# Attention beside an MLP on one core: one visit of the small tiles per slot, and q and k fetched by squares of 32

## The chip, the cores and the metric

The kernel runs on one core of a Trainium2 chip. A core has a matrix engine (TensorE, in the profile PE, with its weight loads as PEld), three other compute engines (VectorE = DVE, ScalarE = ACT, GpSimd = POOL), SyncE (SP), whose queue issues nearly all DMAs here, and 16 DMA engines. The metric is the time of one execution on the device in microseconds; the kernel before has a median of 1464.3 us in 11 runs, from 1461.86 to 1468.6.

## The reference

Eight batches, 12 heads, 448 tokens, head width 64. q and k are normalised by their root mean square along the head width and multiplied by a vector each; then ordinary attention; then an MLP without bias, whose activation is h - tanh(h).

```python
def rmsnorm(x, g):
    rms = np.sqrt(np.mean(x * x, axis=-1, keepdims=True) + 1e-06)
    return x / rms * g
q_n, k_n = (rmsnorm(q, g_q), rmsnorm(k, g_k))
scores = 1.0 / np.sqrt(64) * np.matmul(q_n, k_n.transpose(0, 1, 3, 2))
attn = np.exp(scores - np.max(scores, axis=-1, keepdims=True))
attn = attn / (np.sum(attn, axis=-1, keepdims=True) + 1e-09)
x = np.matmul(attn, v)                    # (8, 12, 448, 64) -> (3584, 768)
h = x @ w_in                              # 768 -> 2048
out = (h - np.tanh(h)) @ w_out            # 2048 -> 768
```

All of it is float32. The two weight matrices come as float64 and are rounded to float32 in the kernel.

## The kernel before

The work of attention is cut into 48 steps: 8 batches by 6 pairs of heads. The MLP works on one whole batch at a time. It needs all six pairs of a batch, so it runs one batch behind: while batch b of the MLP is computed, the attention of batch b + 1 is computed in six *slots* (function `slot`, one for each step s). The MLP is a generator, `mlp()`, that issues one matmul at a time; `run(ns)` takes as many matmuls from it as are worth that time. A slot issues a few pieces of attention, calls `run`, issues the next pieces, and so on: the order in which instructions are written down is the order in each engine's queue, and nothing reorders them later. All six slots of a batch run the same amount of the MLP, four gaps (`gap_ns`). The batch's hidden layer (`hidden`) falls into its first three slots, the projection (`project`) into its last three.

The MLP's two products use seven block products instead of eight, each on blocks of half the rows and half the tokens (224): in the hidden layer a product is 6 matmuls of 128x128 by 224 columns, in the projection 8. Each product fills one of three `mm` banks; VectorE, ScalarE and GpSimd add, subtract and apply tanh. From the second batch on the blocks of weights are read back from DRAM through a ring of six places (`ring_load`, L382 and L384), up to five products ahead.

In the steady part, what a slot s does for attention is spread over four steps:

- **fetch** (L99 to L114, SP's queue): q and k of step s + 4, v of step s + 2. A partition holds several rows of q in one piece of 1024 bytes; k comes in pieces of 256 bytes, three rows to a partition and a rest of 64 rows that is loaded twice.
- **norm**, step s + 3: squares on ScalarE (L119, L120); sums on VectorE (L129, L130); power -1/2 on GpSimd (L131), 8 columns for q and 8 for k; q is scaled on VectorE (L400). k is not: its factor is the `scale` of the exp later.
- **turn**, step s + 2: 8 transposes on TensorE (L411 for k, L415 for q) into two banks, and two copies on ScalarE (L413, L419) to kT and qT.
- **scores** of step s + 1 (L438) and their exp on ScalarE (L443). There are three chunks of 128 keys (0, 1, 2) and one of 64 (`KF`); two heads sit in two halves of the rows of TensorE, 64x128 tiles. Chunks 0 and 1 are in a visit at the slot's start; `KF` and chunk 2 in the middle of the slot.
- **values and sums** of step s, in the same middle visit: last keys (L477, 64x32 tiles), sums of probabilities (L510), values of three chunks (L489, 128x32 tiles), reciprocal (L515) and division (L523) on VectorE.

A *visit* is a stretch in which TensorE is taken from the MLP's 128x128 tiles to smaller ones. Scores, sums and values share five `sc` banks (sc_157 to sc_161 in the rows below), taken in turn; a bank is free when ScalarE or VectorE has read it. The probabilities of a step are also added up on VectorE (`add`, L459 and L460, `add_last`, L467), so that the sums need four matmuls.

Of the kernel before, what the change touches and what calls it, by code (L numbers as in the profile page):

```python
# [91 lines left out]

def fetch(nc, name, t, pair):

# [9 lines left out]
    if name == "v":  # L104
        last = t[:, :, KF]
        nc.sync.dma_start(
            out=t[:, :, :KF].rearrange("p h c d -> p h (c d)"), in_=full.rearrange("h p c d -> p h (c d)")
        )
    else:
        last = t[:, KF]  # L110
        for h in range(2):
            nc.sync.dma_start(out=t[:, :KF, h], in_=full[h])
# [21 lines left out]
def bounded_path(tc, ctx, q, k, v, moe_w_in, moe_w_out, out, g_col, ident, ones, half_ones, neg_half, early):  # L134
# [69 lines left out]
    def load(s, names):  # L204
        b, hp = steps[s]
        for name in names:
            src = {"q": q, "k": k, "v": v}[name]
            if s == 0 and name != "v":
                t = early[name]
            else:  # L210
                shape = [CP, 2, NCH, D] if name == "q" else [P, NCH, 2, D] if name == "k" else [P, 2, NCH, D]
                t = nat.tile(shape, F32, name=f"{name}_nat", bufs=3 if name == "v" else 2)
                fetch(nc, name, t, src[b, 2 * hp : 2 * hp + 2])
            loaded[name, s] = t
# [191 lines left out]
    def turn(s, tk, tq):  # L406
# [13 lines left out]
        turned[s] = rr, kT, qT  # L420

    def sc_bank():
        return bank_of("sc")

    def scores(s, c):
# [16 lines left out]
        for h in range(2):  # L442
            nc.scalar.activation(  # L443
                p[:, h, c if c < 2 else 0, :], tiles[h][:, :n], AF.Exp, scale=rr[:, 0, 2 * c + h : 2 * c + h + 1]
            )
# [221 lines left out]
    def store(b, n, y):  # L667
# [4 lines left out]
        o = part("th").rearrange("p f s -> p (f s)")  # L672
        nc.vector.transpose(out=o, in_=y.rearrange("r (c p) -> r p c", c=NCH))
        for i in range(P // BL):
# [41 lines left out]
    def project_first(b):  # L716
# [35 lines left out]
        wp_stack.close()  # L752
        late["tg"] = pool("tg", bufs=1)

    def mlp():
# [64 lines left out]

    def slot(s):
        gap = gap_ns(s)
        if s < 2 * NP:
            totals(s, sc_bank())
        if has(s + 1):
# [12 lines left out]
        if has(s + 1):  # L838
            scores(s + 1, KF)
        dn = sc_bank() if s >= 2 * NP else None  # L840
        av = [sc_bank() for _ in range(2)]
        last_values(s, av)
        if s >= 2 * NP:
            totals(s, dn)
        divide(s, values(s, av))
        if has(s + 1):
            scores(s + 1, 2)
        for work, n in ((add, 1), (add_last, 1), (norm, 3), (norm_q, 3)):
            run(gap / 2)
            if has(s + n):  # L850
                work(s + n)

    load(0, "qk")
    load(1, "qk")
# [4 lines left out]
    for s in range(NP, NS):  # L859
        slot(s)  # L860
    run(1e9)
# [345 lines left out]
```

## Time and profile before

| | |
|---|---|
| median of 11 runs | 1464.3 us |
| the profiled execution | 1465.15 us, span 1463.4 us |
| PE busy | 1430.6 us, 10272 matmul records |
| DVE, ACT, POOL busy | 818.1, 456.3, 511.6 us |
| DMA | 267895 packets, 250.74 MB, mean 171 GB/s |
| packets under 512 B | 164724 |

The page has the busy time of each engine, a chain of work that ended last (followed back from the last instruction), groups of instructions by line with their mean time, and DMA issues. A float32 matmul appears as two records of the same line. In a row of groups the fields are line, engine, operation, output and inputs, shapes, count, then busy us and the mean of one in ns, then the idle time in front of it and what ended it. In a row of the timeline or the chain they are start and length in us.

### The profile page before, as it was taken

How to read it: one execution, taken by the hardware profiler on the slowest of the kernel's cores; microseconds unless marked ns; L12 is line 12 of the kernel's file. 1: busy time of each engine (PE TensorE's matmuls, PEld its weight loads, DVE VectorE, ACT ScalarE, POOL GpSimd, SP SyncE). 2: the span in 40 equal slices, each digit the busy share in tenths (PEclk: the TensorE clock that was granted, in tenths of full speed). 3: DMA queues.
4: the chain of work that ended last, by engine and by line, in shares of the span. 5: the costliest groups of instructions: out<-in, count | busy, mean ns of one | idle time of the engine just before them, and what ended most of it. 6: DMA issues, size and time to landing. Idle time of an engine off the chain costs nothing.

```text
span 1463.4 us, 26034 instructions
## 1 busy us (share of the span) xinstructions
PE 1430.6 (98%) x10272; PEld 1187.5 (81%) x10272; DVE 818.1 (56%) x1246; ACT 456.3 (31%) x850; POOL 511.6 (35%) x378
## 2 busy tenths in 40 slices
PE   6999899999999999999999999999999999999997
PEld 3568654488888888888888888888888888889997
DVE  4999888755553665347535554555554366433322
ACT  6755453233222332223322233213322233201100
POOL 4656465224331334214422243322433133312310
PEclk9999899999999999999999999999999999999999
DMA  8769778855566555655555545555546654555663
GB/s 188 172 186 265 246 191 225 228 171 156 167 161 171 165 151 160 173 155 155 175 161 163 162 150 177 160 142 170 172 151 165 168 163 139 149 164 162 183 193 98
DMA packets 267895, 250.74 MB, mean 171 GB/s; under 512 B 164724, under 2 KB 210036, under 8 KB 267764
## 3 DMA queue, kind: packets, MB, share of 16 engines
q1 hardware_dynamic: 267760, 248.97, 59.8%
q8 instruction: 84, 1.38, 0.4%
q14 instruction: 47, 0.39, 0.1%
q10 hardware_dynamic: 4, 0.00, 0.0%
HBM read 215.48 MB, written 33.42 MB: 170 GB/s over the span
## 4 chain that ended last, share of the span: by engine, by line
PE 91%; DVE 3%; DMA 2%; ACT 2%; SPq 1%; issue 1%; POOL 0%; ACTq 0%; DVEq 0%
PE mm L578 65%; PE sc L438 9%; PE sc L489 6%; PE mm L743 4%; PE sc L510 2%; PE sc L477 1%; PE sc L411 1%; PE sc L415 1%; DMA w_raw<-in_moe_w_out_dram 1%; DVE rs L515 1%; DVE w_out L82 1%; PE mm L489 0%; DMA q_nat<-in_q_dram 0%; ACT p L443 0%; DMA k_nat<-in_k_dram 0%
## 5 line engine op out<-in xcount | busy, mean ns | idle before, releaser
L578 PE MATMUL mm<-xT,w_f 128*128 128x224 f32 x1392 | 278.8, 355 | 0.0
L578 PEld LDWEIGHTS mm<-xT,w_f 128*128 128x128 f32 x1392 | 260.3, 190 | 16.9 <-issue 9.8
L578 PEld LDWEIGHTS mm<-gT,w_f 128*128 128x128 f32 x1344 | 251.4, 190 | 22.5 <-issue 15.3
L578 PE MATMUL mm<-gT,w_f 128*128 128x224 f32 x1344 | 267.7, 355 | 0.0
L131 POOL TENSOR_TENSOR rr<-rr,neg_half 112x8 f32<-112x8 f32 x96 | 156.5, 1650 | 204.8 <-DVE rr L130 202.9
L615 POOL TENSOR_TENSOR gT<-s,th 128x448 f32<-128x448 f32 x96 | 121.0, 1265 | 297.5 <-ACT th L614 296.8
L578 PE MATMUL mm<-tt,w_f 128*128 128x224 f32 x1044 | 211.2, 354 | 0.0
L578 PEld LDWEIGHTS mm<-tt,w_f 128*128 128x128 f32 x1044 | 196.1, 190 | 7.8 <-issue 7.8
L578 PE MATMUL mm<-tg,w_f 128*128 128x224 f32 x1008 | 200.4, 353 | 0.0
L578 PEld LDWEIGHTS mm<-tg,w_f 128*128 128x128 f32 x1008 | 189.5, 190 | 0.0
L438 PE MATMUL sc<-qT,kT 64*128 64x448 f32 (+1 forms) x960 | 172.4, 503 | 12.0 <-ACT p_last L443 8.5
L443 ACT ACTIVATE p<-sc,rr 128x448 f32<-128x448 f32 x192 | 106.0, 638 | 203.5 <-PE sc L438 203.5
L538 POOL TENSOR_TENSOR tt<-xT,tt 128x224 f32<-128x224 f32 x23 | 31.3, 1363 | 290.8 <-DVE xT L523 290.8
L438 PEld LDWEIGHTS sc<-qT,kT 64*128 64x128 f32 (+1 forms) x960 | 62.9, 167 | 80.4 <-issue 62.0
L515 DVE RECIPROCAL rs<-sc 128x224 f32<-128x224 f32 x42 | 65.4, 1557 | 77.5 <-PE sc L510 77.4
L443 ACT ACTIVATE p_full<-sc,rr 128x448 f32<-128x448 f32 x96 | 55.9, 631 | 144.1 <-PE sc L438 144.1
L614 ACT ACTIVATE th<-s 128x448 f32<-128x448 f32 x96 | 55.4, 577 | 100.7 <-DVE s L640 55.6
L489 PE MATMUL sc<-p,v_nat 128*32 128x224 f32 x1344 | 79.1, 353 | 0.0
L743 PE MATMUL mm<-gT,w_out 128*128 128x448 f32 x192 | 77.0, 558 | 0.0
L697 DVE TENSOR_TENSOR s<-mm,s 128x224 f32<-128x224 f32 x21 | 8.2, 391 | 116.8 <-PE mm L578 109.4
L443 ACT ACTIVATE p_last<-sc,rr 128x224 f32<-128x224 f32 x96 | 37.8, 447 | 114.4 <-PE sc L438 114.4
L523 DVE TENSOR_TENSOR xT<-sc,rs 64x224 f32<-64x224 f32 x168 | 65.3, 389 | 10.3 <-PE sc L489 2.2
(123 smaller groups left out, 1631.7 us busy)
## 6 DMA issues: line engine op xcount, KB each, us to landing
w_f<-w_in SPq DMA_DIRECT2D x196, 384.0 KB, 3.5
w_f<-w_out SPq DMA_DIRECT2D x147, 512.0 KB, 4.2
w_raw<-in_moe_w_out_dram SPq DMA_DIRECT2D x16, 768.0 KB, 5.1
out_dram<-th SPq DMA_DIRECT2D x192, 56.0 KB, 2.0
q_nat<-in_q_dram SPq DMA_DIRECT2D x47, 224.0 KB, 4.4
v_nat<-in_v_dram SPq DMA_DIRECT2D x48, 192.0 KB, 3.7
k_nat<-in_k_dram SPq DMA_DIRECT2D x94, 96.0 KB, 2.8
w_in<-w_out SPq DMA_DIRECT2D x21, 384.0 KB, 6.2
```

The lines of the kernel that those rows point to most:

```text
L131: nc.gpsimd.tensor_tensor(out=r, in0=r, in1=neg_half[:rows], op=ALU.pow)
L438: nc.tensor.matmul(tiles[h][i * keys : (i + 1) * keys, :n], lhsT=kT[r, c * P : c * P + keys], rhs=qT[r, i * n : (i + 1) * n], start=True, ...
L443: nc.scalar.activation(p[:, h, c if c < 2 else 0, :], tiles[h][:, :n], AF.Exp, scale=rr[:, 0, 2 * c + h : 2 * c + h + 1])
L489: nc.tensor.matmul(av[n][r : r + BL, :HS], lhsT=v_nat[:, h, c, m * BL : (m + 1) * BL], rhs=p[c][:, h, n * HS : (n + 1) * HS], start=False, ...
L510: nc.tensor.matmul(dn[r : r + BL, :HS], lhsT=by[n], rhs=moving[2 * n + h], start=(i == 0), stop=(i == len(parts) - 1),)
L515: nc.vector.reciprocal(rs, dn[:, :HS])
L523: nc.vector.tensor_tensor(out=x[m * D : (m + 1) * D, n * HS : (n + 1) * HS], in0=av[n][m * D : (m + 1) * D, :HS], in1=rs[n * D : (n + 1) * ...
L538: eng.tensor_tensor(out=t2, in0=x22, in1=t1, op=ALU.subtract)
L578: nc.tensor.matmul(bank[:, f * HS : (f + 1) * HS], lhsT=w[:, c * width + f, :], rhs=moving[p](c), start=(first and f == 0 and c == 0), sto ...
L614: nc.scalar.activation(th, h, AF.Tanh, bias=0.0, scale=1.0)
L615: eng.tensor_tensor(out=g[:, rows, cols], in0=h, in1=th, op=ALU.subtract)
L743: nc.tensor.matmul(bank[:, :S], lhsT=w_out_row(f, n // HC)[:, n % HC * P : (n % HC + 1) * P], rhs=g[:, f, :], start=(f == 0), stop=(f == C ...
```

## The change

Two things.

*One visit.* From the third batch's attention on (slots 12 to 47), the new function `slot` issues all four score chunks of step s + 1, the values and sums of step s, in one visit: `KF`, then last keys, sums and values, then chunks 0, 1 and 2. The other pieces follow, with the same four gaps of the MLP between them, cut differently. Slots 6 to 11 keep the old order (`early_slot`).

*Squares.* From the fourth batch on (steps 18 to 47), q and k of a step lie in one tile of 128 partitions by 2 by 14 by 32. Partition group 2h + m (32 partitions) holds half m of the head width of head h; a partition is a token within a block of 32, and there are 14 blocks. It is fetched by eight DMAs of 32x14x32, whose pieces are 128 bytes long. Squares are one instruction on ScalarE (896 columns). VectorE sums 28 groups of 32 columns, copies the other half's sums across (four copies of 32x28), adds, and GpSimd takes the power of 128x28. Then VectorE scales q and k together and turns them with two transposes of 32x32 blocks, which give qT and kT; ScalarE multiplies kT by the vector. k now carries its factor, so the exp's scale is 1. Tokens lie in their natural order, so v is fetched by rows in that order too (two DMAs with pieces of 256 bytes), and the transpose in `store` reads its input straight.

TensorE's queue before, from the turn in a hidden-layer slot up to the middle visit (mm are the MLP's banks, tg its sums of blocks):

```order
L438 MATMUL sc_157<-qT,kT 128x448
L438 MATMUL sc_158<-qT,kT 128x448
L578 MATMUL mm_163<-gT,w_f 128x224 x8
L578 MATMUL mm_164<-tg,w_f 128x224 x6
L411 MATMUL sc_159<-ident,k_nat 128x128 x4
L415 MATMUL sc_160<-ident,n 128x112 x4
L578 MATMUL mm_164<-tg,w_f 128x224 x2
L578 MATMUL mm_162<-tg,w_f 128x224 x8
L578 MATMUL mm_163<-gT,w_f 128x224 x4
L438 MATMUL sc_161<-qT,kT 64x224
L438 MATMUL sc_157<-qT,kT 64x224
```

and now, from the middle of the one visit to the MLP behind it (line numbers of the changed kernel; L551 are the values, L499 the scores):

```order
L572 MATMUL sc_161<-rows,ones 32x224 x4
L551 MATMUL sc_157<-p,v_nat 32x224 x8
L551 MATMUL sc_157<-p_full,v_nat 32x224 x4
L551 MATMUL sc_158<-p,v_nat 32x224 x8
L551 MATMUL sc_158<-p_full,v_nat 32x224 x4
L499 MATMUL sc_159<-qT,kT 128x448
L499 MATMUL sc_160<-qT,kT 128x448
L499 MATMUL sc_161<-qT,kT 128x448
L499 MATMUL sc_157<-qT,kT 128x448
L499 MATMUL sc_158<-qT,kT 128x448
L499 MATMUL sc_159<-qT,kT 128x448
L640 MATMUL mm_164<-xT,w_f 128x224 x2
```

The transposes are gone from the queue, and chunks 0, 1 and 2 stand right behind the values, on the banks of the sums and values of the same visit.

VectorE's queue in a hidden-layer slot before, around the norm (s_ and tg are tiles of the MLP):

```order
L129 TENSOR_REDUCE rr<-n 112x8
L130 TENSOR_SCALAR rr<-rr 112x8
L129 TENSOR_REDUCE rr<-sq 128x8
L130 TENSOR_SCALAR rr<-rr 128x8
L634 TENSOR_TENSOR s_4977<-mm_164,s_4975 128x448
L400 TENSOR_TENSOR n<-q_nat,rr 112x2x4x64
```

and now:

```order
L452 TENSOR_REDUCE rr_mine<-qk_n 128x28
L454 COPY rr_other<-rr_mine 32x28 x4
L455 TENSOR_TENSOR rr_mine<-rr_mine,rr_other 128x28
L456 TENSOR_SCALAR rr_mine<-rr_mine 128x28
L698 TENSOR_TENSOR s_4867<-mm_164,s_4866 128x448
L529 TENSOR_TENSOR rows<-rows,p_last 64x2x224 x2
L677 TENSOR_TENSOR gT<-mm_162,th 128x2x224
L464 TENSOR_TENSOR qk_n<-qk_nat,rr_mine 128x896
L706 TENSOR_TENSOR s_4867<-mm_163,s_4867 128x448
L474 STREAM_TRANSPOSE qT<-qk_n 128x448
```

More of the MLP's additions stand between the sums and the scaling, and the transposes of qT (and, further on, kT) stand among them.

The diff, cut to what the prediction speaks of:

```diff
+    if in_order:
+        for h in range(2):
+            nc.sync.dma_start(out=t[:, h, :KF], in_=pair[h, : KF * P].rearrange("(c p) d -> p c d", p=P))
+    elif name == "v":
...
+    def load_blocks(s):
+        b, hp = steps[s]
+        t = loaded["qk", s] = late["blocks"].tile([P, 2, NJ, BL], F32, name="qk_nat", bufs=2)
+        for i, src in enumerate((q, k)):
+            for h in range(2):
+                rows = src[b, 2 * hp + h].rearrange("(j t) (m d) -> m t j d", t=BL, d=BL)
+                for m in range(2):
+                    r = (2 * h + m) * BL
+                    nc.sync.dma_start(out=t[r : r + BL, i], in_=rows[m])
...
+    def norm_blocks(s):
+        mine, other = (late["blocks"].tile([P, 2 * NJ], F32, name=name, bufs=2) for name in ("rr_mine", "rr_other"))
+        nc.vector.reduce_sum(mine, normed[s].rearrange("p i j d -> p (i j) d"), axis=AX.X)
+        for g in range(P // BL):
+            nc.vector.tensor_copy(out=other[g * BL : (g + 1) * BL], in_=mine[(g ^ 1) * BL : ((g ^ 1) + 1) * BL])
...
+        nc.gpsimd.tensor_tensor(
+            out=mine, in0=mine, in1=neg_half[:, :1].to_broadcast([P, 2 * NJ]), op=ALU.pow
+        )
...
+    def scale_blocks(s):
...
+    def turn_blocks(s, i):
+        n = normed[s][:, i].rearrange("p j d -> p (j d)")
+        if i == 0:
+            qT = qkp.tile([P, S], F32, name="qT")
+            nc.vector.transpose(out=qT, in_=n)
...
+        nc.vector.transpose(out=kT, in_=n)
+        nc.scalar.mul(kT, kT, g_col)
...
-        nc.vector.transpose(out=o, in_=y.rearrange("r (c p) -> r p c", c=NCH))
+        nc.vector.transpose(out=o, in_=y if b >= FIRST else y.rearrange("r (c p) -> r p c", c=NCH))
...
+    def slot(s):
+        gap = gap_ns(s)
+        if has(s + 1):
+            scores(s + 1, KF)
+        dn = sc_bank()
+        av = [sc_bank() for _ in range(2)]
+        last_values(s, av)
+        totals(s, dn)
+        divide(s, values(s, av))
+        if has(s + 1):
+            for c in range(KF):
+                scores(s + 1, c)
+        if has(s + 2):
+            load(s + 2, "v")
+        if by_blocks(s + 3):
+            load_blocks(s + 3)
+        blocks = by_blocks(s + 2)
+        run(gap / 2)
+        if has(s + 1):
+            add(s + 1)
+        if blocks:
+            square_blocks(s + 2)
+        run(gap / 2)
+        if blocks:
+            norm_blocks(s + 2)
+        elif has(s + 2):
+            turn(s + 2, sc_bank(), sc_bank())
...
+        run(gap / 2)
+        if has(s + 1):
+            add_last(s + 1)
+        run(gap / 2)
+        if blocks:
+            scale_blocks(s + 2)
...
+        run(gap / 2)
+        if blocks:
+            turn_blocks(s + 2, 0)
+        run(gap / 2)
+        if blocks:
+            turn_blocks(s + 2, 1)
...
+        run(gap)
...
-        slot(s)
+        (early_slot if s < 2 * NP else slot)(s)
```

46 lines of the change are left out of this document (37 added, 9 removed).

## The prediction

> **What bounds the kernel now.** I read the page first: busy time by engine and the chain that ended last.
>
> ```profile
> span 1463.4 us, 26034 instructions
> PE 1430.6 (98%) x10272; PEld 1187.5 (81%) x10272; DVE 818.1 (56%) x1246; ACT 456.3 (31%) x850; POOL 511.6 (35%) x378
> PE 91%; DVE 3%; DMA 2%; ACT 2%; SPq 1%; issue 1%; POOL 0%; ACTq 0%; DVEq 0%
> ```
>
> TensorE is busy for 98% of the span and is 91% of the chain. An average hides stages, so next the stretches: four slots in the middle of the kernel, inside the part that the change touches.
>
> ```profile
> core 0: us, PE busy (x) PEld busy (x) DVE busy (x) ACT busy (x) POOL busy (x), PEclk, DMA share, GB/s
> 780.00:896.00 116.00, 116.00 (x851) 99.88 (x850) 63.85 (x101) 34.87 (x68) 36.71 (x27) 1.00 0.56 161
> ```
>
> TensorE has no idle time at all in 116 us, at full granted clock; VectorE is busy 55%, ScalarE 30%, GpSimd 32%, the DMA engines 56%. In this stage a microsecond taken off TensorE's stream is a microsecond of the span, as long as nobody else becomes late. So I read one slot in the chain of waits (start us, length us, work, matmul records):
>
> ```profile
> 783.81 1.71 PE sc L438 x8
> 785.51 5.49 PE mm L578 x28
> 791.01 0.44 PE sc L411 x4
> 791.45 0.39 PE sc L415 x4
> 791.83 5.31 PE mm L578 x28
> 797.14 0.54 PE sc L438 x8
> 797.68 0.54 PE sc L477 x16
> 798.22 0.52 PE sc L510 x8
> 798.74 2.27 PE sc L489 x48
> 801.01 0.95 PE sc L438 x4
> 801.96 10.79 PE mm L578 x56
> 812.75 1.71 PE sc L438 x8
> ```
>
> One slot is 812.75 - 783.81 = 28.94 us and only TensorE is on it: scores of two key chunks (1.71), transposes of k and q (L411, L415: 0.83), the long visit (last keys' scores, last values, sums, values, third chunk's scores: 4.82) and 112 matmul records of the MLP (21.6). 28 records take 5.31 us, so a record is 0.19 us.
>
> **Removed from TensorE.** The transposes go in slots 16 to 45, which prepare steps 18 to 47: 30 slots x 0.83 = 24.9 us. I take all of it, because the row behind them (791.83) starts with their end.
>
> The merging removes no matmul. The four-record piece, one pair of chunk scores with one entry and exit, takes 0.95; the eight-record piece takes 1.71. The second pair inside a visit therefore costs 0.76, and the entry and exit 0.95 - 0.76 = 0.19. One visit less is worth 0.19 us in each of slots 12 to 46: 35 x 0.19 = 6.7 us. Below, it is worth nothing if the cost belongs to each change of tile shape inside the long visit; above, not more than the 0.19. I take 0.19.
>
> **Added wait 1: banks.** Scores use five banks in turn. In the long visit they go: last keys A, B; sums C; values D, E; then the three chunks on A B, C D, E A. Before, the first two chunks had a visit to themselves with four banks long free. Who frees them:
>
> ```profile
> 797.73 0.78 ACT L443 ACTIVATE p_last<-sc,rr 128x224 f32<-128x224 f32 x2 [4.15 <-PE sc L438]
> 798.80 1.56 DVE L515 RECIPROCAL rs<-sc 128x224 f32<-128x224 f32 x1 [2.75 <-PE sc L510]
> 800.50 1.65 DVE L523 TENSOR_TENSOR xT<-sc,rs 64x224 f32<-64x224 f32 x4
> 784.85 2.21 ACT L443 ACTIVATE p<-sc,rr 128x448 f32<-128x448 f32 x4 [9.74 <-PE sc L438]
> ```
>
> Put on the clock of this slot, chunk 0 starts at 801.01, where values end; A and B were emptied by 798.51. Chunk 1 starts at 801.77: C is free at 800.36, D after two of the four divisions, 801.33. Chunk 2 wants to start at 802.53: E is free at 802.15, 0.38 us early. Its second matmul needs A again, that is the first exp of chunk 0. The visit at 783.81 shows that exp starting 1.04 us after the scores and taking 2.21 / 4 = 0.55: done at 801.01 + 1.59 = 802.60, 0.07 late. Lower bound 0; upper bound 0.6 if ScalarE has one more exp or tanh of that length in front. Nearest to the row is 0.1: 35 x 0.1 = 3.5 us back.
>
> **Added wait 2: the norms on VectorE and GpSimd.** The rows of the old way, and of operations like the new ones:
>
> ```profile
> L131 POOL TENSOR_TENSOR rr<-rr,neg_half 128x8 f32<-128x8 f32 x48 | 79.3, 1653 | 0.3 <-DVE rr L130 0.3
> L537 POOL TENSOR_TENSOR tt<-xT 128x224 f32<-128x224 f32 x23 | 15.2, 659 | 0.0
> L129 DVE TENSOR_REDUCE rr<-sq 128x8 f32<-128x512 f32 x48 | 32.5, 677 | 1.8 <-ACT sq L120 1.8
> L400 DVE TENSOR_TENSOR n<-q_nat,rr 112x512 f32<-112x512 f32 x47 | 44.6, 949 | 9.1 <-POOL rr L131 8.5
> L673 DVE STREAM_TRANSPOSE th<-s 128x448 f32<-128x448 f32 x48 | 45.1, 939 | 11.9 <-ACT s L749 10.5
> 819.30 0.62 DVE L634 TENSOR_TENSOR s<-mm,s 128x448 f32<-128x448 f32 x1 [4.67 <-PE mm L578]
> 811.87 0.17 DVE L130 TENSOR_SCALAR rr<-rr 128x8 f32<-128x8 f32 x1
> 813.10 0.68 DVE L400 TENSOR_TENSOR n<-q_nat,rr 112x512 f32<-112x512 f32 x1
> 729.68 1.62 DVE L400 TENSOR_TENSOR n<-q_nat,rr 112x512 f32<-112x512 f32 x1
> ```
>
> VectorE now sums 896 columns (677 x 896 / 512 = 1.18 us), does six tiny operations (0.17 each, 1.0), scales 896 columns (0.68 to 1.62 for 512, so 1.2 to 2.8) and transposes twice (0.94 each): 5.3 to 6.9 us against 2.7 before. Its 55% becomes 65 to 70%; that average is no bound. ScalarE saves the copy of qT, and stays under a third.
>
> The power is the open price: 28 columns instead of two instructions of 8. By instruction it is 1.65 us, by column 1.65 x 28 / 8 = 5.8. A 224-column subtraction on GpSimd takes only 0.66, so the 1.65 for 8 columns is hardly a start-up cost; I take 5.5. It does not delay TensorE directly. Behind it: VectorE's scaling waits for it, VectorE's queue behind the scaling holds the additions that empty the MLP's banks, and those TensorE needs.
>
> In program order, with half a gap = 14 records = 2.65 us, the norm stands 5.3 us behind the visit and the scaling at 10.6. On average the sums start at 5.0 and the power at 7.2; it ends at 12.7, so VectorE stands about 2 us, and the scaling ends at 13.9 to 15.5. An MLP addition (0.62) due about 11.7 is then done 2.8 to 4.4 us late. Three MLP banks: a bank is wanted again two products later, in the hidden layer (12 records each) 2 x 2.28 = 4.56 us, in the projection (16 records) 6.1. So it is covered on average, and a product that ends badly waits about 1 us. Bounds: 0, and 1 us in each of the 15 slots that run the hidden layer; I take 0.3 x 15 = 4.5 us. If that cover were gone, the whole stall of VectorE would be TensorE's (first rival). kT is ready at about 19 of 21.2 us before the next visit asks for it.
>
> **The fetch.** Per slot, SP issues eight DMAs of 448 pieces of 128 bytes for q and k instead of five, and v's main fetch becomes two DMAs of 256-byte pieces.
>
> ```profile
> L676 SPq DMA_DIRECT2D out_dram<-th x192: 316/478/1700, 208.8 to 1458.7; - x192
> L112 SPq DMA_DIRECT2D k_nat<-in_k_dram x94: 567/612/1415, 6.4 to 1197.3; - x94
> out_dram<-th SPq DMA_DIRECT2D x192, 56.0 KB, 2.0
> k_nat<-in_k_dram SPq DMA_DIRECT2D x94, 96.0 KB, 2.8
> 1452.00:1454.00 2.00, 2.00 (x12) 2.00 (x11) 0.69 (x2) 0.00 (x0) 0.00 (x0) 1.00 0.75 115
> 706.00:708.00 2.00, 2.00 (x12) 2.00 (x12) 0.11 (x1) 1.76 (x4) 0.69 (x1) 1.00 0.50 114
> ```
>
> The stores of the output have the same shape: 448 pieces of 128 bytes, 0.48 us to issue, 2.0 to land. Where only they move (1452 to 1454), 0.75 x 2 us x 16 engines = 24 engine-us carry 230 KB, about 1800 pieces: 13 ns each. Where fetches of k in 256-byte pieces move (706 to 708), 16 engine-us carry 228 KB, 890 pieces: 18 ns. 3584 pieces at 13 to 18 ns are 47 to 65 engine-us per slot; free are 0.44 x 28.94 x 16 = 204. The issues take 8 x (0.48 to 0.61) = 3.8 to 4.9 us, plus up to 2.5 for v, and queued behind them on SP are the weight loads of the MLP. They stand right behind the visit, so SP works on them while TensorE is in its 6.3 us without need of weights, and loads are asked for up to five products (11 us) ahead. I take nothing; the cost without that cover is the third rival.
>
> **The sum**, against the profiled execution (1465.15 us, the span 1463.4 and 1.75 around it): 1465.15 - 24.9 - 6.7 + 3.5 + 4.5 = 1441.5. That execution lies 0.85 above the median of the 11 runs, 1464.3, so 1441 for a median. A new slot should be 28.94 - 0.83 - 0.19 + 0.1 + 0.15, about 28.2 us.
>
> **The rivals.**
>
> *VectorE is late (slower).* The power takes 5.8 us, waits up to 4 us behind GpSimd's subtractions for gT, and the scaling takes 2.8 as at 729.68. The power then ends near 17, the scaling near 20, and an addition due at 11.7 is 8.9 us late: 4.4 beyond the cover, 15 x 4.4 = 66 us: 1465.15 - 24.9 - 6.7 + 3.5 + 66 = 1503. It decides from a lateness of about 6.7 us, where 15 slots lose the 32 gained. For it: L400 has already waited for the power, 8.5 us in all. Against it: that is under 0.2 us a slot, with only half a gap between power and scaling, where there are now two.
>
> *The banks set the pace (no change).* ScalarE empties a pair in 1.1 us, TensorE fills one in 0.76. If it is behind at the visit's end, with other work in front of the first exp, the last pair loses up to 0.9: 35 x 0.9 = 31.5, and 1465. For it: three pairs now come at once. Against it: five of the six banks are free in time by the rows above.
> The Trainium skill (TensorEngine Tiling (Array Packing), PSUM Bottleneck) warns of this: small tiles speed up TensorE but not the emptying of its banks, which may become the limit. By that rule the merged visit gives back what it saves; the rows give it 0.07 us.
>
> *Short pieces cost more to read than to write (slower).* The DMA engines fill up from (204 + 28 of the old fetches) / 3584 = 65 ns a piece. At 80 ns a slot needs (259 - 28 + 287) / 16 = 32.4 us, where 259 is the 56% of now: 30 x 3.4 above today, 1567. Against it: 13 and 18 ns.
> The Trainium skill (DMA: Bandwidth & Descriptors, Specifications) speaks against the change here: transfers of at least 512 B are needed for line rate, below that there is a read-modify-write. The rows of 128 bytes agree that line rate is missed (115 GB/s at 0.75 share), but a slot has room for it.
>
> *Merging is worth nothing*: each change of tile shape keeps its price, 1465.15 - 24.9 + 3.5 + 4.5 = 1448.
>
> **How the numbers follow.** The forecast has 0.64, its own range 1432 to 1457 (both waits at 0, 1433.5; both near their upper bounds). Merging worth nothing 0.12; late VectorE 0.11; banks 0.08; short pieces 0.05. Within 0.2% (2.9 us, about what can be told from no change) lies most of the banks' case: 0.06. Faster: 0.64 + 0.12 + 0.02 = 0.78. Slower: 0.16. The range 1431 to 1460 leaves out the two slow cases and most of the banks'.
>
> **What would show it.** Slots of about 28.2 us in the chain, with no transposes from slot 16 on and one visit of about 6.4 us; TensorE still without idle time. Right on the banks: chunk 2 follows chunk 1 within 0.1 to 0.2 us. Wrong on VectorE: waits of MLP matmuls for additions behind the scaling, or a power far from 5.5 us. Wrong on the fetch: matmuls waiting for weight loads, or a DMA share near 1. An idle TensorE of over 1 us per slot would overturn the forecast.

## The result, and the profile after

The changed kernel takes 1429.51 us (median of 8 runs, 1426.72 to 1436.29) against 1463.4 us before (median of 31 runs, 1460.47 to 1468.6): a ratio of 0.9772, 95% interval 0.9759 to 0.9785. That is 33.9 us less, where 1441 was forecast; the sign was right, the size too small, and the time lies 1.5 us below the range. The profiled execution took 1429.04 us.

The head of the page after: span, and busy time of each engine with its share of the span and its instructions.

```profile
span 1427.2 us, 25681 instructions
PE 1394.7 (98%) x10032; PEld 1172.9 (82%) x10032; DVE 867.8 (61%) x1396; ACT 412.4 (29%) x790; POOL 531.0 (37%) x348
```

TensorE is as busy as before, 98%, and 35.9 us shorter. VectorE went from 56 to 61%, GpSimd from 35 to 37%, ScalarE from 31 to 29%. The same stretch in the middle as before, with the columns of busy time by engine, granted clock, DMA share and GB/s:

```profile
780.00:896.00 116.00, 116.00 (x842) 102.36 (x841) 74.74 (x124) 30.64 (x62) 52.06 (x30) 1.00 0.64 172
```

There is still no idle time on TensorE in 116 us. Nothing that the change added reaches it here. So the gain must be in the slot itself; the chain of waits after, from one visit to the next (start us, length us, work, records; L499 are scores, L539 last keys, L572 sums, L551 values, L640 the MLP):

```profile
738.84 0.54 PE sc L499 x8
739.38 0.54 PE sc L539 x16
739.91 0.52 PE sc L572 x8
740.43 2.27 PE sc L551 x48
742.70 2.60 PE sc L499 x12
745.29 21.38 PE mm L640 x112
766.68 0.54 PE sc L499 x8
```

A slot is 766.68 - 738.84 = 27.84 us, against 28.94 before and the 28.2 expected. Read in the same way, slot 12 is 28.83, slots 13 to 15 are 28.77 or 28.78, slot 16 (the first that prepares a step by squares) is 27.93, and each of the 29 slots behind it, 17 to 45, is 27.84 or 27.85. The gain is 1.10 us in each of them, in hidden-layer slots and projection slots alike:

| TensorE in one slot, us | before | after |
|---|---|---|
| transposes of k and q | 0.83 | 0 |
| visits (scores, values, sums) | 1.71 + 4.82 = 6.53 | 6.47 |
| 112 records of the MLP | 5.49 + 5.31 + 10.79 = 21.59 | 21.38 |
| slot | 28.94 | 27.84 |

The line on the MLP is the surprise: the same 112 records are 0.2 us shorter. In the rows of before, 28 records behind a visit take 5.49 and 28 behind the turn take 5.31; 56 behind the other visit take 10.79, which is 0.17 more than twice 5.31. The first matmuls behind *each* visit are late by 0.17 to 0.18, and that price, too, is now paid once in a slot instead of twice.

From the first score matmul of slot 12 to the end of the span, before has 1463.4 - 291.83 = 1171.6 us and after 1427.2 - 289.48 = 1137.7, which is 33.9 less. The further 2.3 us by which the two spans differ lie ahead of slot 12, in code that the change leaves as it was; in the profiled executions of eleven kernels that are alike up to there, slot 12 starts between 288.1 and 294.4 us.

The new work on VectorE, GpSimd and ScalarE, by groups (busy us, mean ns of one | idle time in front and its releasers):

```profile
L452 DVE TENSOR_REDUCE rr_mine<-qk_n 128x28 f32<-128x896 f32 x30 | 32.0, 1066 | 0.0
L457 POOL TENSOR_TENSOR rr_mine<-rr_mine,neg_half 128x28 f32<-128x28 f32 x30 | 145.1, 4837 | 256.0 <-DVE rr_mine L456 256.0
L464 DVE TENSOR_TENSOR qk_n<-qk_nat,rr_mine 128x896 f32<-128x896 f32 x30 | 46.4, 1546 | 39.3 <-POOL rr_mine L457 36.7 <-DMA w_f<-w_out 2.6
L474 DVE STREAM_TRANSPOSE qT<-qk_n 128x448 f32<-128x448 f32 x30 | 19.1, 638 | 0.5
L504 ACT ACTIVATE p<-sc 128x448 f32<-128x448 f32 x120 | 55.5, 548 | 109.1 <-PE sc L499 109.1
L504 ACT ACTIVATE p<-sc,rr 128x448 f32<-128x448 f32 x72 | 39.8, 643 | 21.9 <-PE sc L499 21.9
```

The power takes 4.84 us, the sums 1.07, the transposes 0.64. VectorE does stand in front of the scaling for the power, 36.7 us in 30 steps or 1.2 us a step, yet the MLP's matmuls between 500 and 1300 us wait for nobody. The two rows of exp are one operation on one shape: with the factor of k as a column of scales 643 ns, with the constant 1, which the squares make possible, 548.

### The profile page after: what moved, and what is told of

Read it like the earlier page. It is cut to its first block, busy times and chain, and to the rows that moved or that the text cites. A ratio compares the mean times of both kernels' runs of the same rounds, so it can differ in the third digit from the quotient of the medians.

```text
span 1427.2 us, 25681 instructions
## 1 busy us (share of the span) xinstructions
PE 1394.7 (98%) x10032; PEld 1172.9 (82%) x10032; DVE 867.8 (61%) x1396; ACT 412.4 (29%) x790; POOL 531.0 (37%) x348
## 4 chain that ended last, share of the span: by engine, by line
PE 92%; DVE 3%; DMA 2%; SPq 1%; issue 0%; ACT 0%; POOL 0%; ACTq 0%
PE mm L640 66%; PE sc L499 10%; PE sc L551 6%; PE mm L805 4%; PE sc L572 2%; PE sc L539 2%; DMA gT<-in_moe_w_in_dram 1%; DMA w_raw<-in_moe_w_out_dram 1%; DVE w_out L82 1%; DVE rs L577 1%; PE mm L551 1%; DMA q_nat<-in_q_dram 0%; PE sc L419 0%; DVE w_out L78 0%; PE mm L572 0%
## 5 line engine op out<-in xcount | busy, mean ns | idle before, releaser
L640 PE MATMUL mm<-xT,w_f 128*128 128x224 f32 x1392 | 275.6, 354 | 0.0
L640 PEld LDWEIGHTS mm<-xT,w_f 128*128 128x128 f32 x1392 | 262.1, 190 | 9.1 <-issue 7.8
L640 PE MATMUL mm<-gT,w_f 128*128 128x224 f32 x1344 | 263.0, 354 | 0.0
L640 PEld LDWEIGHTS mm<-gT,w_f 128*128 128x128 f32 x1344 | 252.8, 190 | 11.4 <-issue 7.2
L457 POOL TENSOR_TENSOR rr_mine<-rr_mine,neg_half 128x28 f32<-128x28 f32 x30 | 145.1, 4837 | 256.0 <-DVE rr_mine L456 256.0
L640 PE MATMUL mm<-tt,w_f 128*128 128x224 f32 x1044 | 208.7, 353 | 0.0
L640 PEld LDWEIGHTS mm<-tt,w_f 128*128 128x128 f32 x1044 | 197.0, 190 | 3.9 <-issue 3.9
L640 PE MATMUL mm<-tg,w_f 128*128 128x224 f32 x1008 | 197.7, 352 | 0.0
L640 PEld LDWEIGHTS mm<-tg,w_f 128*128 128x128 f32 x1008 | 190.6, 190 | 0.0
L499 PE MATMUL sc<-qT,kT 64*128 64x448 f32 (+1 forms) x960 | 167.7, 499 | 12.2 <-ACT p_last L504 8.6
L499 PEld LDWEIGHTS sc<-qT,kT 64*128 64x128 f32 (+1 forms) x960 | 70.9, 167 | 83.9 <-issue 49.6
L600 POOL TENSOR_TENSOR tt<-xT,tt 128x224 f32<-128x224 f32 x23 | 17.1, 745 | 230.4 <-DVE xT L585 230.4
L504 ACT ACTIVATE p<-sc 128x448 f32<-128x448 f32 x120 | 55.5, 548 | 109.1 <-PE sc L499 109.1
L135 POOL TENSOR_TENSOR rr<-rr,neg_half 112x8 f32<-112x8 f32 (+1 forms) x36 | 59.6, 1678 | 57.1 <-DVE rr L134 57.0
L551 PE MATMUL sc<-p,v_nat 128*32 128x224 f32 x1344 | 79.1, 353 | 0.0
L464 DVE TENSOR_TENSOR qk_n<-qk_nat,rr_mine 128x896 f32<-128x896 f32 x30 | 46.4, 1546 | 39.3 <-POOL rr_mine L457 36.7
L805 PEld LDWEIGHTS mm<-gT,w_out 128*128 128x128 f32 x192 | 36.4, 193 | 37.3 <-issue 36.3
```

What stands on the lines that cost most here:

```text
L135: nc.gpsimd.tensor_tensor(out=r, in0=r, in1=neg_half[:rows], op=ALU.pow)
L457: nc.gpsimd.tensor_tensor(out=mine, in0=mine, in1=neg_half[:, :1].to_broadcast([P, 2 * NJ]), op=ALU.pow)
L464: nc.vector.tensor_tensor(out=n.rearrange("p i j d -> p (i j) d"), in0=loaded.pop(("qk", s)).rearrange("p i j d -> p (i j) d"), in1=rr[:, ...
L499: nc.tensor.matmul(tiles[h][i * keys : (i + 1) * keys, :n], lhsT=kT[r, c * P : c * P + keys], rhs=qT[r, i * n : (i + 1) * n], start=True, ...
L504: nc.scalar.activation(p[:, h, c if c < 2 else 0, :], tiles[h][:, :n], AF.Exp, scale=1.0 if rr is None else rr[:, 0, 2 * c + h : 2 * c + h ...
L551: nc.tensor.matmul(av[n][r : r + BL, :HS], lhsT=v_nat[:, h, c, m * BL : (m + 1) * BL], rhs=p[c][:, h, n * HS : (n + 1) * HS], start=False, ...
```

## The experiments

The theory with which I went to the chip: the gain is made of three parts, 0.83 us per slot for the transposes, 0.17 for one visit instead of two (0.39 saved, less a wait for banks), and 0.09 because the constant scale lets ScalarE give the banks back sooner; the norms and the short pieces cost nothing. Rivals: the squares alone bring all of it, or less than the transposes; the norms have ample room, or none; the fetch is near its limit. The kernel before was timed beside each kernel; its median in the four groups of runs was 1463.1 to 1465.7. No kernel leaves anything out.

**One visit alone.** All steps keep the old fetch, norm and turn.

```diff
-    FIRST, NJ = 3, S // BL
+    FIRST, NJ = B, S // BL
```

> One visit from slot 12 on, but q and k of all batches fetched, normed and turned the old way. Theory: a removed visit is worth 0.20 us where the MLP comes back (its 112 records took 21.59 us a slot before, 21.39 after) plus 0.19 in the visits, less a wait of about 0.22 for banks, as slots 12 to 15 of the changed kernel show (28.77 us against 28.94): 35 x 0.17 = 6 us less than before, about 1457.5 us, slots of 28.77. Rival 1, the prediction's own sum (0.19 less 0.1): 3 us less, 1460. Rival 2, everything beyond the 24.9 us of the transposes is the merging's: 9 us less, 1454.5.

Measured: 1456.71 us, ratio 0.9948 (0.9929 to 0.9967). The chain of waits of one slot (the turn, between the two pieces of the MLP, is left out here):

```profile
495.90 0.54 PE sc L499 x8
...
499.76 2.69 PE sc L499 x12
502.45 5.49 PE mm L640 x28
...
508.77 15.90 PE mm L640 x84
524.67 0.54 PE sc L499 x8
```

A slot is 28.77, 0.17 less than before. The MLP's records take 5.49 + 15.90 = 21.39: one late start, not two, 0.20 saved. The visit takes 502.45 - 495.90 = 6.55 against 6.53. Its three chunks take 2.69, where the prediction's prices make 0.95 + 2 x 0.76 = 2.47; the 0.22 is the loss by the wait for banks, and it eats the 0.19 that the visit saves within itself. So merging is worth what the MLP's side saves: 35 x 0.17 = 6.0 us.

**Squares alone.** Slots 12 to 47 have two visits as before, but norm, scaling and turns are done by squares.

```diff
         if has(s + 1):
-            scores(s + 1, KF)
...
+            scores(s + 1, 0)
+            scores(s + 1, 1)
...
+        run(gap)
+        if blocks:
+            scale_blocks(s + 2)
+        if has(s + 1):
+            scores(s + 1, KF)
+        dn = sc_bank()
+        av = [sc_bank() for _ in range(2)]
+        last_values(s, av)
+        totals(s, dn)
+        divide(s, values(s, av))
+        if has(s + 1):
+            scores(s + 1, 2)
         run(gap / 2)
...
+        if blocks:
+            turn_blocks(s + 2, 0)
...
         if blocks:
-            scale_blocks(s + 2)
+            turn_blocks(s + 2, 1)
```

> Squares from the fourth batch on, but two visits in every slot, as before the change. Theory: 30 slots lose the 0.83 us of transposes and nothing else, 24.9 us less than before, about 1438.5 us, slots of 28.11 us; VectorE's and GpSimd's longer norms cost nothing. Rival 1, the norms do cost and merging repays it: 20 us less or fewer. Rival 2, the squares save more than the transposes: 28 us less, 1435.5.

Measured: 1450.04 us, ratio 0.9906 (0.9887 to 0.9924): 11.5 above what I expected. Projection slots are 28.10, which is 28.94 - 0.84, as they should be; most groups of three hidden-layer slots take 86.85 to 86.90 instead of 3 x 28.10 = 84.3. The chain of waits shows why; from the sums of squares of a step to the scores that need its kT:

```profile
500.14 1.00 DVE rr_mine L452
...
502.46 4.80 POOL rr_mine L457
...
507.28 2.02 DVE qk_n L464
509.30 1.48 DVE rs L577
...
521.27 0.56 DVE kT L478
...
521.85 0.68 ACT kT L479
...
522.57 1.77 PE sc L499 x8
```

Power, scaling, then the reciprocal and the divisions of the middle visit behind the scaling on VectorE, then the turn of k, and the scores at 522.57 wait for kT. In this kernel the norm stood too near the scaling for the visit between. Whether the squares are worth less than the transposes, or my placing of them was bad, this run leaves open; hence the next one.

**Squares alone, with the norm half a slot earlier.** As the one before, but the squares and the norm of step s + 3 follow the middle visit, and the scaling and the turns follow in the next slot.

```diff
         run(gap / 2)
         if blocks:
-            square_blocks(s + 2)
+            scale_blocks(s + 2)
         run(gap / 2)
         if blocks:
-            norm_blocks(s + 2)
+            turn_blocks(s + 2, 0)
...
+        if by_blocks(s + 3):
+            square_blocks(s + 3)
         run(gap / 2)
-        if blocks:
-            turn_blocks(s + 2, 0)
         if has(s + 1):
             add_last(s + 1)
+        if by_blocks(s + 3):
+            norm_blocks(s + 3)
```

> Squares only, two visits in every slot as in the earlier run of squares alone, but each step's norm is made half a slot earlier: sums and power behind the middle visit, scaling and transposes at the start of the next slot, three half gaps apart instead of two, and kT three half gaps and a visit ahead of its use instead of two half gaps. Theory: the 12 us missing there were VectorE's chain through power, scaling, division and transposes, which gave kT 1.1 to 1.3 us late to the next slot's first scores; with room, all slots take 28.11 and the run is 24.9 us below the kernel before, about 1438.5. Rival: the longer norms need the free stretch that one visit leaves; two visits lose about 10 us wherever the norms stand, 1448 or more.

Measured: 1441.57 us, ratio 0.9853 (0.9835 to 0.987). In the chain of waits every slot of that part is now 28.10 or 28.11 us, hidden layer or projection:

```profile
729.74 0.54 PE sc L499 x8
...
734.56 10.79 PE mm L640 x56
...
747.05 10.79 PE mm L640 x56
757.84 0.54 PE sc L499 x8
```

So the squares are worth 0.84 us a slot, the transposes and nothing else: 30 x 0.84 = 25.2 us. By the medians it is 22.2 us, and the interval, 19 to 24, does not hold the 25.2; in the two traces the stretch from the values of slot 11 to those of slot 47 is 25.1 us shorter (1014.2 instead of 1039.3). What the times lack against that must lie outside this stretch or in the spread between executions; which of the two is not shown. The loss of the run before was its placing. Two visits and two late starts of the MLP (10.79 twice) are still there.

**Exp with a column of ones as its scale**, in the changed kernel: the same result, but ScalarE reads the scale from a column again.

```diff
-                scale=1.0 if rr is None else rr[:, 0, 2 * c + h : 2 * c + h + 1],
+                scale=ones[:, :1] if rr is None else rr[:, 0, 2 * c + h : 2 * c + h + 1],
```

> The changed kernel, but the exp takes its scale from a column of ones also where the squares would let it take the constant 1. Theory: the last pair of scores waits for the first exp of the visit, and an exp with a column takes 0.64 us instead of 0.55; the twelve records of chunk scores go from 2.60 to 2.69 us, a slot from 27.84 to 27.93: 30 x 0.09 = 2.7 us more, about 1432. Rival: the pair waits for VectorE's divisions alone, 2.60 stays, no change.

Measured: 1430.25 us, ratio 0.9769 (0.9746 to 0.9793). Against after that is 0.7 us more by the medians, within the noise of the times; the trace decides. The group of the exps, and then the three chunks in the chain of waits of this kernel:

```profile
L504 ACT ACTIVATE p<-sc,ones 128x448 f32<-128x448 f32 x120 | 66.2, 634 | 103.8 <-PE sc L499 103.8
```

```profile
742.93 2.69 PE sc L499 x12
```

The exp is 0.09 longer, the chunks take 2.69 instead of 2.60, and all slots are 27.93 or 27.94. What ScalarE loses on its first exp TensorE loses in full: the wait for banks is a wait for ScalarE, and the constant scale is worth 30 x 0.09 = 2.7 us.

**Fetch twice.** Each of the eight DMAs of q and k is issued a second time, into a tile that nobody reads.

```diff
-                    nc.sync.dma_start(out=t[r : r + BL, i], in_=rows[m])
+                    for dst in (t, more):
+                        nc.sync.dma_start(out=dst[r : r + BL, i], in_=rows[m])
```

> The changed kernel with each of the eight fetches of q and k issued twice, the second into a tile that nobody reads. Theory: the fetch is covered with room for as much again: within 3 us of 1429.5, with a DMA share higher by about a tenth in the slots. Rival, short pieces come near the limit of the DMA engines or of SP's queue: matmuls wait for weight loads, some 30 x 1 us or more.

Measured: 1429.65 us, ratio 0.9768 (0.9749 to 0.9787), slots 27.84 or 27.85. The stretch in the middle, with the columns as above:

```profile
780.00:896.00 116.00, 116.00 (x842) 102.36 (x841) 74.14 (x125) 30.61 (x62) 51.58 (x30) 1.00 0.73 190
```

The share goes from 0.64 to 0.73. In a slot that is 0.09 x 27.84 x 16 = 40 engine-us for 3584 more pieces, about 11 ns each. The fetch has room even twice over.

**The power twice**: a second power of the same 28 columns stands in front, its result unused.

```diff
-        nc.gpsimd.tensor_tensor(
-            out=mine, in0=mine, in1=neg_half[:, :1].to_broadcast([P, 2 * NJ]), op=ALU.pow
-        )
+        more = late["blocks"].tile([P, 2 * NJ], F32, name="rr_more", bufs=1)
+        for dst in (more, mine):
+            nc.gpsimd.tensor_tensor(
+                out=dst, in0=mine, in1=neg_half[:, :1].to_broadcast([P, 2 * NJ]), op=ALU.pow
+            )
```

> The changed kernel with one more power of 128x28 on GpSimd in front of the one that is used (4.84 us more, its result unused). Theory: an addition of VectorE may be late by two products of the MLP (4.56 us in the hidden layer, 6.1 in the projection) before TensorE waits; the scaling ended 11.9 us behind the visit and would end at 16.7, so additions are up to 6 us late: TensorE loses about 1.5 us in each of the 15 hidden-layer slots and little in the others, 10 to 25 us in all, 1440 to 1455. Rival 1, VectorE's queue is no matter to TensorE: within 3 us of 1429.5. Rival 2, no cover: 30 x 4.84 = 145 us more.

Measured: 1507.76 us, ratio 1.0309 (1.0285 to 1.0333): 78 us lost for 4.84 us more of GpSimd in a step. Projection slots stay at 27.84. The hidden-layer slots of a batch become about 32.8, 31.6 and 34 to 35, together 15 to 16 us too long; five batches make 78. The chain of waits of one of them:

```profile
656.05 4.80 POOL rr_more L459
...
660.91 4.80 POOL rr_mine L459
...
666.74 0.63 DVE s L708
...
667.41 7.25 PE mm L642 x28
```

It is the path that the prediction named for its first rival: power, scaling, an MLP addition behind the scaling in VectorE's queue, TensorE. But two of the three slots lose about 4.84 us or more, up to 7.3, as if nothing of it were covered. The last row shows what else there is: 28 records take 7.25 us, where they take 5.31 to 5.49 elsewhere. The granted clock of TensorE, the column in front of the DMA share, is lower behind the wait than in front of it:

```profile
660.00:662.00 2.00, 2.00 (x13) 2.00 (x12) 0.00 (x0) 0.00 (x0) 1.92 (x2) 1.00 0.74 194
670.00:672.00 2.00, 2.00 (x6) 1.78 (x6) 1.90 (x3) 1.55 (x3) 1.59 (x2) 0.50 0.00 0
672.00:674.00 2.00, 2.00 (x12) 1.98 (x11) 1.08 (x1) 0.00 (x0) 2.00 (x2) 0.99 0.90 236
```

TensorE had stood for 3.2 us, counted from the time at which its next record was due; behind that ten records come 0.37 us apart instead of 0.19. In the whole trace TensorE stands 57 us in 20 waits, and the records behind these waits take 21 us more than 0.19 each; together these are the 78. All ten waits of 3.2 us and more are followed by the lower clock, none of the ten of 2.0 us and less. So about a quarter of the loss is not waiting, but clock that the waiting cost. Also without that part I had expected far more cover than there is. How much there is, the next run measures.

**The power longer by a third**: eight columns more (1.64 us and an issue), result unused.

```diff
+        more = late["blocks"].tile([P, 8], F32, name="rr_more", bufs=1)
+        nc.gpsimd.tensor_tensor(out=more, in0=mine[:, :8], in1=neg_half, op=ALU.pow)
```

> The changed kernel with one more power of 128x8 on GpSimd in front of the one that is used (about 1.67 us more, its result unused). Theory: an addition behind the scaling was done at 648.1 in a hidden-layer slot of the changed kernel and its bank was wanted near 650.0, so about 1.85 us of cover are left: no slot longer than 27.85 by more than 0.3, within 5 us of 1429.5. Rival: the cover is used up, every microsecond more is paid in the hidden layer: 15 x 1.67 = 25 us more, 1454.

Measured: 1444.17 us, ratio 0.9867 (0.985 to 0.9883): 14.7 more than after, between the two expectations. The chain of waits in one hidden-layer slot:

```profile
536.48 5.00 POOL rr_mine L459
...
541.50 2.01 DVE qk_n L466
543.52 0.55 DVE s L700
...
544.11 4.81 PE mm L642 x24
```

The group of the MLP's matmuls of the hidden layer from 500 to 1300 us (busy us, mean ns | idle time in front, what ended it):

```profile
L642 PE MATMUL mm<-xT,w_f 128*128 128x224 f32 x895 | 180.2, 355 | 9.0 <-DVE s L700 7.1 <-DVE s L698 1.7 <-DVE s L708 0.2
```

The three hidden-layer slots of a batch are 28.0, 28.45 and 29.55: too long by 0.2, 0.6 and 1.7, and over the five batches of the trace by 12.7 us in all. For 1.7 us more of power, this leaves about 1.5, 1.1 and 0 us of cover in the changed kernel. The trace of the changed kernel itself agrees: from the end of the last operation that reads an MLP bank to the first matmul that writes this bank again, the smallest distances in the three slots are 1.7, 1.3 and 0.34 us in most batches. In its tightest slot the norm just fits.

**The same, with the scaling half a gap later.** Kernels of the two runs above, with VectorE's scaling, and the turn of q behind it, moved in the order; GpSimd's order stays.

```diff
         run(gap / 2)
-        if blocks:
-            scale_blocks(s + 2)
...
         run(gap / 2)
         if blocks:
-            turn_blocks(s + 2, 0)
+            scale_blocks(s + 2)
         run(gap / 2)
         if blocks:
+            turn_blocks(s + 2, 0)
             turn_blocks(s + 2, 1)
```

> The longer power of e8 cost 14.7 us, all in hidden-layer slots, and the matmuls there waited for VectorE's additions. This kernel keeps the longer power, but VectorE's scaling and the turn of q stand half a gap (2.65 us) later in the order, so that one more addition of the MLP passes ahead of the scaling. VectorE's order is the cause (theory): the additional 1.7 us are covered again, every slot from 16 on is 27.84 and the time is within 3 us of the changed kernel's 1429.5. Rival, GpSimd itself is the cause, because its own subtractions for the MLP stand behind the longer power and their order has not changed: the time stays near 1444.

> The power twice over, 4.84 us more, as in e3 (1507.8, hidden-layer slots 3.8 to 7 us too long), with VectorE's scaling and the turn of q half a gap (2.65 us) later. Theory (VectorE's order): half a gap more of cover takes away 2.65 us of the loss of each of the 15 hidden-layer slots or a little more, since one addition passes ahead: 1507.8 - 15 x 2.65 = 1468, between 1450 and 1475. Rival (GpSimd's own queue): 1500 to 1508 as before.

Measured: 1438.35 us, ratio 0.982 (0.9797 to 0.9842), and 1490.76 us, ratio 1.0182 (1.0162 to 1.0203). Of the 14.7 us lost to the longer power 5.8 come back, of the 78 lost to the double one 17. Both lie between the theory and its rival. The chain of waits of the first of the two kernels, in the slot that still loses, and the score chunks of another slot:

```profile
511.92 2.01 DVE qk_n L466
513.93 0.55 DVE s L698
...
514.52 1.78 PE mm L642 x8
...
548.09 3.10 PE sc L501 x12
```

Two of the three hidden-layer slots are whole again, 27.84 or 27.85, among them the one that had lost 1.7. The first projection slot is 28.3, since its chunks wait 0.5 longer for banks, which VectorE's divisions empty later there. The middle one went from 28.45 to 29.09; TensorE waits for the same addition (L698) as before, only longer. There the scaling did not wait for the power itself. The timeline of this slot, GpSimd and then VectorE:

```profile
503.05 4.79 POOL L459 TENSOR_TENSOR rr_mine<-rr_mine,neg_half 128x28 f32<-128x28 f32 x1
507.81 3.70 POOL L679 TENSOR_TENSOR gT<-s,th 128x448 f32<-128x448 f32 x3
```

```profile
508.97 1.54 DVE L689 TENSOR_TENSOR tg<-gT 128x448 f32<-128x448 f32 x1 [3.77 <-POOL gT L679]
```

The power ends at 507.84 and the scaling starts at 511.92. Two operations of the MLP (L689, L690) now stand in front of the scaling, and the first of them reads what GpSimd subtracts behind the power: VectorE stands 3.77 us for it. This happens once in each of the five batches, 18.9 us in all in this kernel and 34.6 in the other. So the rival has a part as well, only not on TensorE directly: GpSimd's own queue reaches TensorE through VectorE. VectorE's order decides which work meets the late power; where that work itself waits for GpSimd, moving the scaling gains nothing. Of what the second kernel wins back, a good part is clock and not cover: in its trace TensorE stands 44 us instead of 57, and the records behind the waits are 10 us too long instead of 21. Of its ten waits of 2.3 to 2.4 us, five were followed by the lower clock.

**Both parts from one batch earlier.** q and k tiles of both kinds share memory, so that squares can begin with the third batch's steps and one visit with slot 10.

```diff
-    FIRST, NJ = 3, S // BL
+    FIRST, NJ = 2, S // BL
...
-        (early_slot if s < 2 * NP else slot)(s)
+        (early_slot if s < 2 * NP - 2 else slot)(s)
```

> Squares from the third batch on instead of the fourth, and one visit from slot 10 on instead of 12; the squares' tiles share the memory of the old q and k tiles. Theory: 6 more slots without transposes (6 x 0.83 = 5.0), 2 more with one visit and four with the quicker exp (0.9 together): 6 us less than the changed kernel, about 1423.5. Rival: in slots 10 and 11 VectorE still has the weights of the MLP to prepare and is late with the norms; then half of it or none.

Measured: 1425.86 us, ratio 0.9737 (0.9714 to 0.976), the fastest of all kernels here, and 3.7 us under after (the two ratios make it 5). All slots from 12 on are 27.84 or 27.85. Six more steps at 0.83 + 0.09 and two more merged slots make 5.9; the time agrees with that within its noise.

## Why the prediction was right in direction and wrong in size

Its own sum takes 23.6 us off the profiled execution; measured from slot 12 on are 33.9. Term by term:

| term, us | predicted | measured | by |
|---|---|---|---|
| transposes, 30 slots | -24.9 | -25.2 | slots of 28.10 with squares alone |
| one visit, 35 slots | -6.7 | -13.7 | 35 x (0.19 in the visit + 0.20 on the MLP's side) |
| wait for banks | +3.5 | +5.0 | 30 x 0.13 + 5 x 0.22 |
| norms on VectorE and GpSimd | +4.5 | 0 | no idle time before MLP matmuls |
| fetch | 0 | 0 | nothing changes with twice the fetch |
| sum | -23.6 | -33.9 | |

**Removed from TensorE: transposes.** Right.

**Removed from TensorE: merging.** This step failed, and is the larger half of the miss. The prediction took the entry and exit of a visit from the score pieces alone, 0.95 - 0.76 = 0.19, and wrote "above, not more than the 0.19". The quoted rows held the other half: 5.49 behind a visit against 5.31 behind the turn, for 28 records each. I read the 5.31 for the price of a record and passed over the 5.49. A visit costs 0.39 us, half of it on the small tiles' side and half on the side of the MLP. One visit alone shows the MLP's half, 21.39 instead of 21.59; the other half is hidden there by the wait for banks. The single records of before show both halves in the visit at 783.81: its first record starts 0.28 us behind the last of the MLP, which come 0.19 apart, and the second pair 0.48 behind the first, where the others are 0.376 apart; on the way out it is 0.47 instead of 0.376, and 0.29 instead of 0.19. These are about 0.1 us four times, 0.20 on each side. Around the transposes, on tiles of 128x128 and 112x128, no step is above 0.02. The Trainium skill (TensorEngine Tiling (Array Packing), Key Properties) says that a change of tiling mode drains TensorE; by that rule both ends of a visit have a price, and the trace agrees with about 0.20 us at each.

**Added wait 1: banks.** The mechanism was right: the chunks come in the order of their banks, and chunk 2 waits for the first exp. With the old exp it costs 0.22 a slot, twice my 0.1, as one visit alone shows, and 0.13 with the new one. The lateness itself was close to the 0.07 of the prediction: in the single records the second matmul of chunk 2 starts 0.13 late with the old exp and 0.03 with the new one. But its second record then follows 0.48 us behind its first instead of 0.376, as at the start of a visit; this 0.10 for the broken stream was not in the sum. The quicker exp was missed: the change says that the scale becomes 1, and I costed that at nothing. It is worth 2.7 us, which the 5.0 in the table already contains. The Trainium skill (ScalarE: Activation LUTs, What ACT_TABLE_LOAD costs) has the size of it: an operand that is a column adds about 93 ns to an activation. The trace agrees: 643 - 548 = 95.

**Added wait 2: norms.** The term was mis-sized: 0.3 us in each of 15 slots predicted, 0 measured. The sums took 1.07 instead of 1.18, the power 4.84 instead of 5.5, the transposes 0.64 instead of 0.94 (the price was from one that read strided, this one reads straight), so VectorE stands 1.2 us a step and not 2, and every stall is covered. But the reason was nearer to failing than I thought. The bounds of the term were 0 and 15; 1.7 us more of power already cost 13 to 15. A power at its upper bound of 5.8 us, 0.96 more, would have used up the 0.34 us of the tightest slot and cost about 0.6 us in each batch, 3 us in all (an estimate from these distances). The first rival, VectorE late, is the same mechanism at a longer power, and it came true with 4.84 us more, at 1507.8. That this lies beside the 1503 worked out for a lateness of 8.9 is chance: about 20 of the 78 us lost are the lower clock behind the waits, which the prediction did not have.

**The fetch.** Right. In after, a stretch in which hardly anything but these fetches moves (742 to 744 us) gives this:

```profile
742.00:744.00 2.00, 2.00 (x24) 1.03 (x17) 1.61 (x5) 0.32 (x1) 0.07 (x1) 1.00 0.69 114
```

0.69 x 2 us x 16 engines = 22 engine-us for 228 KB, about 1780 pieces: 12 ns a piece, beside the 13 of the stores. Where the prediction weighed the Trainium skill's (DMA: Bandwidth & Descriptors, Specifications) line of 512 bytes, the trace shows both: 114 GB/s at 0.69 share is a poor rate, and it costs this kernel nothing.

**The other rivals.** Banks setting the pace: no, the whole wait is 0.13 of 27.84. Merging worth nothing: no, a slot with the merging alone is 0.17 shorter. The range missed by 1.5 us because of merging alone: its lower end, both waits at 0 (1433.5), already left the norms free, but it held merging to an upper bound of 0.19 a slot, which the prediction's own rows contradicted.

## What to carry to other kernels

When work on an engine is cut into stretches of different tile shapes, price a change of shape on both sides: compare the first matmuls of the *returning* work behind each kind of interruption, not only the inserted pieces. When a producer feeds a queue that another engine drains in order, its duration is free up to the cover and is paid behind it, here from 0.2 to 1.7 us in a slot for 1.7 us more; a stall that is long enough costs clock on top, here from a wait of 2.3 to 3.2 us on. Before work is moved away from a late producer, look whether what takes its place waits for the same producer. A run with a little more of the producer's work measures the cover, and tells how safe a fit is, which a trace without idle time cannot. And an operand that becomes a constant may be a gain in itself, where the instruction frees a buffer that is waited for.

## What the runs showed of the hardware

- The power on GpSimd goes by columns: 1.65 us for 128x8 and 4.84 for 128x28, that is 0.16 us a column and 0.4 for the rest. Put twice in a row, the second starts 4.86 us behind the first.
- VectorE's scaling of 128x896 takes 1.09 us while GpSimd has nothing, 1.54 beside one of GpSimd's 128x224 subtractions, and 2.01 beside its 128x448 ones; three of these in a row, from the start of the scaling on, take 4.55, 1.5 each in the mean instead of 1.14. In both cases the scaling ends 0.95 us behind the end of the first subtraction beside it (757.18 and 756.23, 843.26 and 842.31), as if most of it had run only then. The timeline of the changed kernel (start us, length us), VectorE and then GpSimd (ahead of the scaling at 783.55 GpSimd ends its power, and starts nothing until it is over):

```profile
755.64 1.54 DVE L464 TENSOR_TENSOR qk_n<-qk_nat,rr_mine 128x896 f32<-128x896 f32 x1 [0.64 <-DMA w_f<-w_out]
783.55 1.09 DVE L464 TENSOR_TENSOR qk_n<-qk_nat,rr_mine 128x896 f32<-128x896 f32 x1 [0.71 <-POOL rr_mine L457]
841.25 2.01 DVE L464 TENSOR_TENSOR qk_n<-qk_nat,rr_mine 128x896 f32<-128x896 f32 x1 [0.97 <-POOL rr_mine L457]
```

```profile
755.57 0.66 POOL L599 TENSOR_TENSOR tt<-xT 128x224 f32<-128x224 f32 x1
841.18 4.55 POOL L677 TENSOR_TENSOR gT<-s,th 128x448 f32<-128x448 f32 x3
```

  The Trainium skill (GPSIMD Engine Reference, Specifications) has the two engines share their SBUF interfaces, with contention where VectorE reads two inputs from there; the trace agrees. A later power does not make this dearer here: in the three hidden-layer slots of a batch the scaling takes 1.09, 2.01 and 2.01 in the changed kernel, and the same with the power longer or twice.
- A transpose of 32x32 blocks of 128x448 takes 0.63 to 0.64 us where it reads its input straight.
- The granted clock of TensorE falls to 0.50 for some 3 to 5 us behind a wait of 3.2 us or more (ten of ten in the run with the power twice), behind waits of 2.3 to 2.4 us in five of ten, and behind none of those of up to 2.1 us in these two runs; records of 128x224 then come 0.37 us apart instead of 0.19.
- Reading pieces of 128 bytes takes 11 to 12 ns of a DMA engine each, hardly less than writing them (13).
